# Turned tiles and decay exponents in one ring of four PSUM banks, and the next batch's q loaded earlier in two halves

## The chip, the cores and the metric

The kernel runs on one NeuronCore of a Trainium2 chip. The metric is device time in microseconds (us): how long one execution takes. A core has five engines that work in parallel, each through its own instructions in order: TensorE (PE in the profile; its weight loads are listed as PEld), VectorE (DVE), ScalarE (ACT), GpSimd (POOL) and SyncE (SP), which here does nothing but issue DMA transfers. Engines wait for each other through semaphores. TensorE writes its results to PSUM, a memory of eight banks of 2 KB per partition; VectorE and ScalarE read them from there.

## The reference

Two blocks follow one another. The first is an mLSTM cell, a recurrence over 768 positions for 4 batches and 8 heads of size 40:

```python
for t in range(S):
    m_new = np.maximum(f_gate[:, :, t] + m, i_gate[:, :, t])
    f_stab = np.exp(f_gate[:, :, t] + m - m_new)
    i_stab = np.exp(i_gate[:, :, t] - m_new)
    m = m_new
    C = f_stab[:, :, None, None] * C + i_stab[:, :, None, None] * np.einsum('bhd,bhe->bhde', vt, kt)
    n = f_stab[:, :, None] * n + i_stab[:, :, None] * kt
    h_tilde = np.einsum('bhde,bhe->bhd', C, qt)
    nq = np.einsum('bhd,bhd->bh', n, qt)[:, :, None]
    denom = np.maximum(np.abs(nq), 1.0)
    o = 1.0 / (1.0 + np.exp(-o_gate[:, :, t]))
    y[:, :, t] = o * h_tilde / denom
```

Its output, seen as 3072 rows of 320 numbers, goes through a layer of eight experts. Each row has one expert, chosen by a hash of its token id, and becomes `np.maximum(x @ w1[e], 0) @ w2[e]`, with 1024 hidden units.

## The kernel before, in words

The recurrence is computed in chunks of 128 positions: 6 chunks (`NB`) for each of 4 batches, so 24 steps `s`, with batch `b = s // 6` and chunk `c = s % 6`. The loop of line 713 issues them in an order written out by hand. The second stage, from line 775 on, runs the experts one after another on TensorE; it gathers its rows from `x_rows`, a buffer in DRAM which every step of the first stage adds 128 rows to.

One step of the loop issues, in this order:

- SyncE's loads: k for step s+3, v for step s+3 (line 164, which waits until the attention of the step before has read that buffer), in some steps a later batch's q (line 182), output gates (line 177), and one slice of expert weights (line 101).
- `decayed`: GpSimd multiplies the state C by its decay.
- `turn_k(s + 2)`: four TensorE transposes of k (line 273) and a ScalarE copy out of PSUM into `kT` (line 274). Then turns of q: `turn_q` does the same for q (lines 286 and 287). In batch 0 these are four turns of batch 0's own q in its first steps, and six turns of the next batch's q. A later batch's q lies in one tile `ql`, whose rows are interleaved, so that all six turns are needed before the first chunk of that batch can be scored. Which turns a step makes is in `first_turns` (batch 0) and `turns_of` (later batches). One step ahead of each turn `pad_q` (line 278) copies its part of `ql` into a padded tile `qp` on VectorE.
- `back(s - 1)` and `finish(s - 1)`: four transposes of the finished heads `hT` into `xo` (line 418), then VectorE and GpSimd scale them (lines 424 to 434).
- `decays(s + 1)`: four matmuls give the exponents `ab` (line 309), which ScalarE exponentiates (line 313); two more give `xb` (line 317), the weight of the state that enters the chunk. VectorE multiplies q by it into `qs` (line 321), ScalarE copies its last column to `dec` (line 323). The operand `R` of these matmuls comes from a DRAM buffer by two small transfers (`load_a`, line 197), issued on SyncE's queue one step ahead.
- `sigmoid` of the output gates on ScalarE, in steps 3, 9, 15 and 21 and once at the start; `state(s)`: sixteen matmul passes (line 376) for the update of C, which VectorE adds; the store of x (line 435); `scores(s + 1)` (line 345) and `weigh(s + 1)` on VectorE; `attend(s)` (lines 396 and 403), whose result ScalarE copies to `hT` (line 411).

In steps 2 to 22 pieces of the routing of tokens to experts lie in between, from step 13 on with matmuls into a tile `tk` (line 582).

All eight PSUM banks are in use: two for `sp0` and `sp1`, two for `ht`, two under the tag `tr` (in which `tr`, `xo`, `xb`, `tk` and some single tiles take turns) and two for `ab`. A tile in a ring of two banks waits until the tile two before it has been read.

## Time and profile before

| what | us |
|---|---|
| median of 3 runs (lowest to highest) | 449.61 (447.66 to 449.61) |
| the profiled execution: its own time | 448.97 |
| its span, first to last instruction | 447.2 |
| of this: attention loop, end of step 0's attention to end of step 23's | 33.3 to 184.0 |
| experts' matmuls | 199.5 to 439.5 |
| TensorE busy | 393.6 (88%) |
| ScalarE, VectorE, GpSimd busy | 136.3, 134.9, 118.5 |

In the chain of work that ended last, TensorE has 74% of the span; ScalarE 6%, DMA transfers 5%, SyncE's queue 3%. The parts of the profile that the prediction rests on are shown there. A timeline row gives the start, the duration, the engine, the line of the kernel, the operation with output and inputs, and in square brackets the engine's idle time before it and what ended that. A row of a table of stretches gives the stretch, its length, the busy time of TensorE, its weight loads, VectorE, ScalarE and GpSimd with their numbers of instructions, the TensorE clock that was granted (1.00 is full speed), the busy share of the 16 DMA engines, and GB/s.

### The profile page before, as it was taken

The page shows a single profiled execution, that of the slowest core. Times are in us where ns is not written, and L with a number is a line of the kernel's source. Part 1 is how long each engine was busy: PE and PEld are TensorE (multiplying, and loading weights), DVE is VectorE, ACT ScalarE, POOL GpSimd, SP SyncE. Part 2 cuts the span into 40 slices and gives each one's busy share as a digit, 9 for nine tenths or more (in the row PEclk, how much of TensorE's full clock was granted, in tenths as well). Part 3 has the DMA queues.
Part 4 walks back from the last instruction along what each step waited for, and adds up shares of the span by engine and source line. Part 5 has one row for each costly group of instructions (what it writes and reads, how often), then busy time and mean ns, then how long its engine had stood idle before and what let it go on. Part 6 is the DMA issues. An engine that isn't in the chain of part 4 may idle for free.

```text
span 447.2 us, 7391 instructions
## 1 busy us (share of the span) xinstructions
PE 393.6 (88%) x2862; PEld 263.8 (59%) x2862; DVE 134.9 (30%) x371; ACT 136.3 (30%) x238; POOL 118.5 (26%) x204
## 2 busy tenths in 40 slices
PE   3367987998899999449999999999999999999993
PEld 2255766776677787325665755655656556565551
DVE  7363544575465666211112011020020110200100
ACT  5248683576358546101111111011011111101110
POOL 6363312131233343171131240311311402011011
PEclk9989997999699999959999999999999999999997
DMA  9829569559847663143751823514417200000000
GB/s 171 208 60 177 113 140 231 108 127 220 190 116 149 141 151 94 46 118 135 250 172 29 262 77 103 177 45 133 150 45 237 88 0 31 13 15 30 1 16 28
DMA packets 111736, 51.37 MB, mean 115 GB/s; under 512 B 86576, under 2 KB 105844, under 8 KB 111700
## 3 DMA queue, kind: packets, MB, share of 16 engines
q1 hardware_dynamic: 105850, 39.31, 36.1%
q0 software_dynamic: 2496, 8.20, 5.8%
q10 hardware_dynamic: 3354, 3.37, 2.3%
q8 instruction: 23, 0.38, 0.4%
q14 instruction: 13, 0.11, 0.1%
HBM read 42.00 MB, written 8.63 MB: 113 GB/s over the span
## 4 chain that ended last, share of the span: by engine, by line
PE 74%; ACT 6%; issue 6%; DMA 5%; SPq 3%; POOL 3%; DVE 1%; ACTq 0%; POOLq 0%; DVEq 0%
PE mh L825 21%; PE zp L854 20%; PE sp L345 6%; PE mh L818 6%; PE ht L403 6%; PE ab L309 3%; PE ht L396 2%; PE xo L418 2%; PE ht L376 2%; ACT kT L274 2%; SPq L101 1%; ACT hT L411 1%; ACT qT L287 1%; PE tk L582 1%; PE tp L801 1%
## 5 line engine op out<-in xcount | busy, mean ns | idle before, releaser
L854 PE MATMUL zp<-w2t,h 128*128 128x320 f32 x384 | 105.2, 433 | 0.0
L825 PE MATMUL mh<-xT,w1t 128*128 128x416 f32 x256 | 97.9, 527 | 0.9 <-issue 0.9
L854 PEld LDWEIGHTS zp<-w2t,h 128*128 128x128 f32 x384 | 72.7, 190 | 32.1 <-issue 3.3
L825 PEld LDWEIGHTS mh<-xT,w1t 128*128 128x128 f32 x256 | 47.5, 193 | 43.8 <-issue 42.7
L807 DVE COPY xT<-tp 128x384 f32<-128x384 f32 x16 | 8.9, 558 | 141.7 <-PE tp L803 124.0
L788 POOL DMA_INDIRECT out_dram<-zo,s_idx x26 | 25.6, 986 | 92.6 <-ACT zo L787 92.6
L834 ACT ACTIVATE h<-mh 128x416 f32<-128x416 f32 x32 | 16.5, 517 | 109.2 <-PE mh L818 59.6
L787 ACT COPY zo<-zp 128x320 f32<-128x320 f32 x26 | 11.1, 425 | 101.1 <-PE zp L854 92.9
L434 POOL TENSOR_TENSOR x<-x,den 128x320 f32<-128x320 f32 x24 | 17.3, 722 | 86.4 <-DVE den L433 48.3
L353 DVE TENSOR_TENSOR w<-sp,w 128x512 f32<-128x512 f32 x48 | 30.9, 686 | 19.1 <-PE sp L345 18.0
L832 DVE TENSOR_SCALAR h<-mh 128x416 f32<-128x416 f32 x32 | 18.9, 592 | 53.4 <-PE mh L825 26.9
L345 PE MATMUL sp<-qT,kT 64*128 64x128 f32 x384 | 31.6, 310 | 3.2 <-ACT qT L287 3.2
L345 PEld LDWEIGHTS sp<-qT,kT 64*128 64x128 f32 x384 | 26.5, 210 | 5.9 <-ACT qT L287 3.6
L313 ACT ACTIVATE w<-ab 128x512 f32<-128x512 f32 x48 | 26.1, 596 | 9.6 <-PE ab L309 9.1
L403 PE MATMUL ht<-w,v 128*64 128x128 f32 x384 | 28.1, 292 | 0.0
L411 ACT COPY hT<-ht 128x512 f32<-128x512 f32 x24 | 14.0, 583 | 43.8 <-PE ht L403 39.8
L818 PE MATMUL mh<-xT,w1c 64*128 64x416 f32 x128 | 26.7, 535 | 0.0
L781 POOL DMA_INDIRECT xg<-x_rows,g_idx x24 | 23.4, 975 | 9.8 <-issue 9.8
L929 POOL COPY hrem<-h 128x256 f32<-128x256 f32 x8 | 3.2, 398 | 83.2 <-ACT h L834 83.2
L403 PEld LDWEIGHTS ht<-w,v 128*64 128x64 f32 x384 | 22.0, 144 | 4.2 <-issue 3.9
L287 ACT COPY qT<-tr 128x512 f32<-128x512 f32 x24 | 22.4, 970 | 5.1 <-PE tr L286 5.1
L286 PE MATMUL tr<-ident,qp 128*128 128x128 f32 x96 | 16.3, 298 | 8.5 <-ACT kT L274 4.4
(177 smaller groups left out, 411.7 us busy)
## 6 DMA issues: line engine op xcount, KB each, us to landing
w2t<-in_moe_w_dram SPq DMA_DIRECT2D x28, 320.0 KB
w1t<-in_moe_w_dram SPq DMA_DIRECT2D x28, 256.0 KB
k<-in_k_dram SPq DMA_DIRECT2D x24, 160.0 KB
v<-in_v_dram SPq DMA_DIRECT2D x24, 160.0 KB
og<-in_o_gate_dram SPq DMA_DIRECT2D x24, 160.0 KB
x_rows<-x SPq DMA_DIRECT2D x24, 160.0 KB
ql<-in_q_dram SPq DMA_DIRECT2D x3, 960.0 KB
w1c<-in_moe_w_dram SPq DMA_DIRECT2D x14, 128.0 KB
```

Source lines behind the costliest of these rows:

```text
L287: nc.scalar.copy(qb[b]["T"][:, :, cols], tp[:])
L313: nc.scalar.activation(w[:, hf], ab[:], AF.Exp)
L345: nc.tensor.matmul(sp[hf][:, j, :], lhsT=d["kT"][r, j, :], rhs=q_of(s)[r, j, :], start=True, stop=True,)
L353: nc.vector.tensor_tensor(d["w"][:, hf], d["sp"][hf][:], d["w"][:, hf], op=ALU.mult)
L403: nc.tensor.matmul(place(j, hf), lhsT=d["v"][:, 2 * j + hf, :], rhs=d["w"][:, hf, j, :], start=(c == 0 and j0 == 0), stop=True, skip_group ...
L411: nc.scalar.copy(d["hT"].rearrange("p f i t -> p f (i t)"), d["ht"][:, :, : 2 * P])
L781: nc.gpsimd.indirect_dma_start(out=xg, out_offset=None, in_=x_d[:, :], in_offset=bass.IndirectOffsetOnAxis(ap=idx, axis=0),)
L788: ins = nc.gpsimd.indirect_dma_start(out=out[:, :], out_offset=bass.IndirectOffsetOnAxis(ap=idx, axis=0), in_=zo[:], in_offset=None, bound ...
L818: nc.tensor.matmul(hp[i][:, :cols], lhsT=w1c[r, fp, :], rhs=xT[r, 2, :cols], start=first, stop=not first,)
L825: nc.tensor.matmul(hp[i][:, :cols], lhsT=w1t[:, db, fb * P : (fb + 1) * P], rhs=xT[:, db, :cols], start=(first and db == 0), stop=(not fir ...
L832: nc.vector.tensor_relu(h[:, 2 * fp, :cols], hp[i][:, :cols])
L854: nc.tensor.matmul(zp[:], lhsT=h[:, fb, j * P : (j + 1) * P], rhs=w[2][:, fb, :], start=(fb == 0), stop=(fb == FB - 1),)
```

## The change

There are four edits. All tiles of the tags `tr` and `ab` share one ring of four banks, in the order in which they are issued. The load of batch b+2's q, 960 KB at chunk 5, becomes two loads of four heads each, at chunks 2 and 4. The turns of q are one per step (in batch 0 two in step 4). And `decays` is cut in two: `entering`, which makes `xb`, `qs` and `dec`, comes after `state`, and `load_a` is written after it.

```diff
-        def load_q(b):
+        def load_q(b, part):
 
-            qb[b] = {"l": ld.tile([P, H, NB * D], F32, name="ql", bufs=2)}
-            nc.sync.dma_start(qb[b]["l"][:], q[b].rearrange("h (p r) d -> p h (r d)", r=NB))
+            if part == 0:
+                qb[b] = {"l": ld.tile([P, H, NB * D], F32, name="ql", bufs=2)}
+            hs = slice(part * PR, (part + 1) * PR)
+            nc.sync.dma_start(qb[b]["l"][:, hs], q[b, hs].rearrange("h (p r) d -> p h (r d)", r=NB))
...
-            tp = ps.tile([P, PR, P], F32, name="tr", tag="tr", bufs=2)
+            tp = ps.tile([P, PR, P], F32, name="tr", tag="tr", bufs=4)
...
-                ab = ps.tile([P, PR, P], F32, name="ab", bufs=2)
+                ab = ps.tile([P, PR, P], F32, name="ab", tag="tr", bufs=4)
...
-            if c > 0:
-                xb = ps.tile([P, PR, P], F32, name="xb", tag="tr", bufs=2)
+
+        def entering(s):
+            d = st[s]
+            R = Rs[s % 2]
+            if s % NB > 0:
+                xb = ps.tile([P, PR, P], F32, name="xb", tag="tr", bufs=4)
...
-        turns_of = {0: (0,), 1: (1, 2), 2: (3,), 3: (4,), 4: (5,)}
-        first_turns = {1: (0,), 2: (1, 2), 3: (3,), 4: (4, 5)}
+        turns_of = {c: (c,) for c in range(NB)}
+        first_turns = {1: (0,), 2: (1,), 3: (2,), 4: (3, 4), 5: (5,)}
...
-        load_q(1)
+        load_q(1, 0)
+        load_q(1, 1)
         gates_turn(g0)
         decays(0)
+        entering(0)
...
-            if c == 5 and b + 2 < B:
-                load_q(b + 2)
+            if c in (2, 4) and b + 2 < B:
+                load_q(b + 2, c // 2 - 1)
...
             if s + 1 < NT:
                 decays(s + 1)
-            if s + 2 < NT:
-                load_a(s + 2, nc.scalar if s == 0 else nc.sync)
...
             state(s)
             if s + 1 < NT:
+                entering(s + 1)
+                if s + 2 < NT:
+                    load_a(s + 2, nc.scalar if s == 0 else nc.sync)
                 k_weights(s + 1)
```

The other tiles of the tag `tr` (`tpg`, `xo`, `cps`, `tk`) get `bufs=4` in the same way.

## The prediction

> **What bounds the kernel now.** I read the slices of the span first, to see where TensorE is not full; the first row's digits are its busy tenths, the second the granted clock, the third the DMA share, 11.2 us per digit.

> ```profile
> PE   3367987998899999449999999999999999999993
> PEclk9989997999699999959999999999999999999997
> DMA  9829569559847663143751823514417200000000
> ```

> From the nineteenth digit on the experts keep TensorE full, which this change does not touch. Inside the loop (fourth to seventeenth digit) the clock falls twice, in the seventh and the eleventh, each time with the DMA share at 9 or 8. The chain of waits says what happens in the first (start, length, what):

> ```profile
> 64.77 0.58 SPq L182
> ...
> 65.39 0.76 SPq L177
> ...
> 66.19 1.84 SPq L177
> ...
> 68.07 3.37 SPq L101
> ...
> 71.49 2.37 DMA R<-decay_pieces
> ...
> 73.90 1.23 PE ab L309 x4
> ...
> 76.37 2.01 PE sp L345 x16
> 78.38 1.92 PE ht L403 x16
> ```

> Line 182 is batch 2's q. Behind it one weight load takes 3.37 us to issue, which took 0.61 to 0.67 in the steps beside it, so the small R transfers go out at 71.49. The matmuls at the end are slow: 2.01 and 1.92 us against 1.09 and 1.05 elsewhere in this chain. The timeline has the waits themselves:

> ```profile
> 71.72 0.33 DVE L278 COPY qp<-ql 128x320 f32<-128x320 f32 x1 [2.87 <-DMA ql<-in_q_dram]
> 72.20 0.63 PE L286 MATMUL tr<-ident,qp 128*128 128x128 f32 x4 [2.52 <-DVE qp L278]
> 73.90 1.23 PE L309 MATMUL ab<-R,L 128*64 128x512 bf16 x4 [0.64 <-DMA R<-decay_pieces]
> ```

> In an ordinary step, what TensorE waits for is ScalarE's copies, ahead of `xo` and of second turns:

> ```profile
> 88.46 0.66 PE L418 MATMUL xo<-ident,hT 128*128 128x128 f32 x4 [0.29 <-ACT kT L274]
> 81.59 0.66 PE L286 MATMUL tr<-ident,qp 128*128 128x128 f32 x4 [0.29 <-ACT kT L274]
> 82.56 0.66 PE L418 MATMUL xo<-ident,hT 128*128 128x128 f32 x4 [0.32 <-ACT qT L287]
> 45.26 0.66 PE L418 MATMUL xo<-ident,hT 128*128 128x128 f32 x4 [0.66 <-ACT qT L287]
> ```

> Last the stretches, cut at the ends of the attention of steps 4 to 12:

> ```profile
> 64.30:69.02 4.72, 4.72 (x65) 3.60 (x65) 2.31 (x7) 2.26 (x4) 1.40 (x2) 1.00 0.94 234
> 69.02:80.30 11.28, 8.11 (x69) 6.95 (x68) 5.09 (x17) 3.46 (x6) 1.86 (x3) 0.70 0.89 199
> 80.30:87.17 6.87, 6.26 (x87) 4.93 (x88) 4.05 (x15) 4.33 (x7) 1.40 (x2) 1.00 0.38 83
> 87.17:93.07 5.90, 5.61 (x83) 4.46 (x84) 3.45 (x11) 3.41 (x6) 2.63 (x5) 1.00 0.47 105
> 98.95:105.76 6.81, 5.63 (x83) 4.49 (x84) 4.10 (x13) 5.56 (x8) 0.72 (x1) 1.00 0.85 178
> 110.50:121.10 10.60, 7.91 (x67) 6.73 (x67) 4.55 (x16) 3.45 (x6) 1.40 (x2) 0.68 1.00 220
> ```

> Steps 6 and 12 (rows 2 and 6) take 11 us where others take 6, and both fill the DMA engines.

> **Part 1: q three steps sooner.** In step 6 three things go: the 2.52 us for the padded q, the 0.64 us for R, and the slow clock. From 73.90 the slow work is 1.23 (ab) + 0.28 (xb) + 0.96 (line 376) + 2.01 + 1.92 = 6.40 us; the same work at full clock, by the chain between 89.12 and 93.07, is 0.55 + 0.22 + 0.45 + 1.09 + 1.05 = 3.36. That is 3.04 us, 6.2 in all. In step 12 the waits are 1.58 and 1.11 and the slow work 6.38, so 5.7. Together 11.9 us, if nothing puts the stall elsewhere. After the change the second half is issued in step 4 (10), at about 58 us in today's clock, and is wanted by `pad_q` at the end of step 5, some 9 us later; today the whole load took 64.77 to 71.7.

> [...] The trace has 2.52 and 0.64 us of idling with 1 us of transposes between, and then 6.4 us at half rate. [...]

> **Part 2: what the halves cost on SyncE's queue.** Each half is one more issue (0.58 us by line 182's row) ahead of gates, weights and R, in steps 2, 4, 8 and 10. What a whole q costs the DMA engines follows from the stretches: steps 11 and 12 together were busy 0.87 × 4.74 + 1.00 × 10.60 = 14.7 us; two steps with their loads but no q (step 10: 0.85 × 6.81 = 5.8) are 11.6; so 3.1 us, 1.55 a half. In step 10 the queue then has 7.3 us of work in a step of about 6.3, and steps 11 and 12 have 5.8 each in about 5.1. A backlog of 1.0, then 1.7, then 2.5 us grows, and R is behind it. R goes in behind v, two gates and weights, 4.3 us of transfers (0.95 + 1.9 + 1.5, from differences between such stretches), lands about 2 us after that (2.37 by the chain, queueing included), and is wanted at 1.6 us into the next step: 6.7 us after its step began. So R is late by about half a us in each of steps 12 and 13, more if the backlog is larger. In steps 2 to 6 the same sum stays just inside. I charge 1.5 us (0 to 6), plus 0.5 for the added issues. Behind a late R on TensorE are C's update and the scores, hence everything.

> [...] I stay with 0.5. The third split, at the start, adds one issue at 13.56, where the next load but one waits till 19.65 anyway: nothing, or 0.5 us.

> **Part 3: ring and turns.** With four banks a tile waits for the fourth before it. `xo` no longer waits for the copy of kT (or of the first qT) but only for `hT`, its own input, which ScalarE has copied 0.65 us after the attention's end, while the transposes of k and q take until 1.04. New waits: the second `ab` tile waits for kT's copy (done at 1.24; it would start at about 1.9), and `xb` for qT's (done at 2.34; it starts at about 2.7, since C's update now precedes it). Both covered by 0.4 us or more; with two turns (step 4) the second `ab` is held 0.3. Full TensorE work of a step with one turn, from the chain: 0.59 + 0.45 + 0.56 + 0.55 + 0.45 + 0.22 + 1.09 + 0.60 + 1.05 = 5.56 us. From the starts of line 403:
> - steps 8 and 9: 5.90 to 5.6, 0.3 each; steps 14 and 15, with `tk` (0.68 more): 6.57 to 6.2, 0.35 each.
> - steps 10 and 16, held by the sigmoid's lateness: `xo` waits for `hT` instead of kT, 0.5 each.
> - steps 7 and 13 lose a second turn: 6.9 to 5.6, 1.3 each.
> - step 2 (three turns of q to two): 7.70 to 6.0; step 3: 6.71 to 6.0; step 4: 7.74 to 7.05; step 1: 0.9, for its third tile no longer waits behind the sigmoid (36.74 in the timeline).
> - steps 5, 11 and 17 gain a turn, and the scores that follow need its copy: 0.45 dearer each.
> - step 0: `xb` waits 3.74 us for kT with 0.81 us of C's update behind it; the update now goes first: 0.8.
> Sum: 0.6 + 0.7 + 1.0 + 2.6 + 1.7 + 0.7 + 0.7 + 0.9 - 1.3 + 0.8 = 8.4 us. Bounds: the unshown waits could take half of it; it cannot exceed TensorE's own work by more than 1.

> **Part 4: the moves.** On VectorE `qs` goes behind C's addition (0.32 us); `qs` is read by the next step's attention, a step away. On ScalarE `dec` goes behind the sigmoid; GpSimd wants it a step later, and line 382's addition waits for that, in steps that wait for the sigmoid anyhow. `load_a` passes nothing on SyncE's queue; in step 0, on ScalarE's, it passes `dec` and one load. I cost all three at nothing; without cover it is 0.3 us a step.

> **Sum.** 11.9 + 8.4 - 2.0 = 18.3 us off the profiled execution's 448.97 (span 447.2): 430.7. The median of the runs is 0.64 above that execution, so about 431.5.

> **Rivals.** (a) The stall only shrinks: the backlog of steps 10 to 12, and likewise 4 to 6, makes R late enough for the clock to fall once more. For it: those steps run the DMA engines at 0.85 to 1.00 already, and the faster loop asks for the same bytes in less time. Against it: the backlog I get is 2.5 us, spread over three steps. Each transition would lose 1.5 + 3.0 again: 440. (b) The shared ring brings nothing, because in place of waits before `xo` come waits before `ab` and `xb` on the same copies: 449.6 - 11.9 + 2 = 440. Against it: the 0.4 us of margin above. (c) Slower: the halves hold R up in all four steps in which they are issued, steps 2, 4, 8 and 10, each at today's price of 5.7 to 6.2 us: 24 us, against 11.9 + 8.4 saved, so 453. [...] (d) The load of q is not what stalls, weights are: then only part 3 counts, 441. Against it: steps 4 and 10 have gates and weights too and do not stall.

> **How the numbers follow.** Likeliest 0.62, 427 to 437; (a) 0.12; (b) 0.08; (c) 0.06; (d) 0.03; better than summed (TensorE gap-free and no late R), 423 to 427, 0.07; the rest 0.02. The range that leaves out less than 2 in 10 is 426 to 441. A measurement of this kernel can tell about 0.5%, 2.2 us, from no change: faster 0.91, within it 0.02, slower 0.07.

> **What would show it.** Right: no wait for `ql` at line 278; the clock at 1.00 in steps 5 to 13; `xo` waiting for `hT` or nothing; steps 6 and 12 at 5 us; the loop's end near 166. Wrong: matmuls of `ab` waiting for R in steps 6, 12 and 13 with a clock below 0.8 after; `ab` or `xb` waiting for kT or qT; a long issue before R in steps 2, 4, 8 or 10.

## The result, and the profile after

The changed kernel takes 430.70 us (median of four runs, 429.59 to 431.33) where the kernel before, run beside it, takes 448.74 (447.66 to 449.61): a ratio of 0.960, with a 95% interval of 0.956 to 0.963. The profiled execution took 429.59 us, its span 427.9 (before: 448.97 and 447.2). The predicted time was 431.5, with a range of 426 to 441.

The slices of the span of the changed kernel, 10.7 us per digit: TensorE's busy tenths, its granted clock and the DMA share.

```profile
PE   2369999999999992599999999999999999999992
PEclk9868999999999998589999999999999999999997
DMA  8929998899676720527616318235216201000000
```

From the fifth digit to the fifteenth TensorE is busy nine tenths of the time or more and its clock does not fall any more, although the DMA engines are busier than before (8 or 9 from the fourth digit to the tenth, where they were 5 to 9). The stretches, cut at the ends of the attention of the steps, have the columns that the prediction's table had (stretch, length, busy time of TensorE, its loads, VectorE, ScalarE, GpSimd, then clock, DMA share and GB/s); these are steps 6, 8, 12 and 13:

```profile
65.24:70.08 4.84, 4.84 (x68) 3.98 (x68) 3.79 (x14) 3.24 (x6) 1.83 (x3) 1.00 0.98 199
75.81:81.26 5.45, 5.45 (x85) 4.41 (x84) 3.57 (x12) 3.24 (x6) 2.63 (x5) 1.00 0.90 213
97.86:103.13 5.27, 5.00 (x68) 4.16 (x68) 3.23 (x13) 3.39 (x6) 1.41 (x2) 1.00 0.95 198
103.13:109.37 6.24, 5.81 (x85) 4.57 (x83) 4.58 (x14) 3.48 (x6) 2.49 (x4) 1.00 0.94 229
```

Step 6 fell from 11.19 us to 4.84, step 12 from 10.69 to 5.27, and step 8, an ordinary one, from 5.90 to 5.45 with TensorE busy in all of it. Steps 12 and 13 are not full: 0.27 and 0.43 us of them are idle.

The timeline of TensorE in the changed kernel (start, duration, line, operation, and in brackets an idle time and what ended it) shows what is left of the waits. The rows without brackets are step 9's `xo` and `xb`, which wait for nothing now. The others are waits that remain: `ab` behind two turns in step 4, the scores behind the added turn in steps 5 and 11 (and 17), and R in steps 12 and 13.

```profile
55.67 0.41 PE L311 MATMUL ab<-R,L 128*64 128x512 bf16 x2 [0.46 <-ACT qT L289]
...
62.46 1.16 PE L351 MATMUL sp<-qT,kT 64*128 64x128 f32 x16 [0.29 <-ACT qT L289]
...
82.12 0.60 PE L424 MATMUL xo<-ident,hT 128*128 128x128 f32 x4
...
83.59 0.41 PE L323 MATMUL xb<-R,Lx 128*64 128x512 bf16 x2
...
95.08 1.16 PE L351 MATMUL sp<-qT,kT 64*128 64x128 f32 x16 [0.26 <-ACT qT L289]
...
99.59 0.77 PE L311 MATMUL ab<-R,L 128*64 128x512 bf16 x4 [0.27 <-DMA R<-decay_pieces]
...
105.22 0.77 PE L311 MATMUL ab<-R,L 128*64 128x512 bf16 x4 [0.28 <-DMA R<-decay_pieces]
```

Of the signs that the prediction named, those for being right came: no wait for `ql`, the clock at 1.00 in steps 5 to 13, steps 6 and 12 near 5 us, the loop's end at 163.67. Two of those for being wrong came as well, in small: R is late in steps 12 and 13, but with no fall of the clock behind it, and `ab` waits for a copy of its ring, of kT in step 1 (0.83 us) and of qT in step 4 (0.46 us).

The chain of waits of the changed kernel (start, length, what) says why R is late in step 13. It is the last load of step 12 on SyncE's queue: v (line 164), two gates (line 177) and a weight slice (line 101) are issued first, and it goes out 4.3 us after that step began.

```profile
97.86 0.60 PE tr L275 x4
98.46 0.09 SPq L164
...
98.60 1.33 SPq L177
...
99.98 1.42 SPq L177
...
101.44 0.69 SPq L101
...
102.17 3.00 DMA R<-decay_pieces
...
105.22 0.66 PE ab L311 x4
```

**Where the time went.** The intervals between the ends of the attention give the loop: from 33.26 to 183.99 before, from 33.33 to 163.67 now, 150.73 us against 130.34. These 20.4 us are more than the span gained (19.3), because the part from the loop's end to the end of the span grew from 263.2 to 264.2. Its first group of expert matmuls is the place; from the timelines, the changed kernel first and then the one before:

```profile
179.17 5.74 PE L834 MATMUL mh<-xT,w1t 128*128 128x416 f32 x8 [0.90 <-POOL xT L896]
```

```profile
199.51 4.78 PE L825 MATMUL mh<-xT,w1t 128*128 128x416 f32 x8 [0.90 <-issue]
```

The same eight matmuls took 5.74 us instead of 4.78, for the clock, which had fallen while TensorE waited for the gathered rows, came back later in them: 5.4 us after their start instead of 3.5. In the stretches of these matmuls (the changed kernel, then the one before) the granted clock was 0.53 and 0.63:

```profile
179.17:184.91 5.74, 5.74 (x10) 2.92 (x11) 0.00 (x0) 0.00 (x0) 3.16 (x4) 0.53 0.72 251
```

```profile
199.51:204.29 4.78, 4.78 (x10) 2.54 (x11) 0.00 (x0) 0.00 (x0) 3.14 (x4) 0.63 0.92 287
```

This is not a price of the change: in the experiments below the same group takes anything from 4.62 us (the last of them) to 5.76 (q loaded whole), and the last section shows at which moments the clock changed.

### The profile page after: what moved, and what is told of

Same layout as the page of the kernel before. It is cut to its first block, busy times and chain, and to the rows that moved or that the text cites. A ratio compares the mean times of both kernels' runs of the same rounds, so it can differ in the third digit from the quotient of the medians.

```text
span 427.9 us, 7402 instructions
## 1 busy us (share of the span) xinstructions
PE 386.1 (90%) x2862; PEld 258.5 (60%) x2862; DVE 136.1 (32%) x371; ACT 134.6 (31%) x238; POOL 118.7 (28%) x204
## 3 DMA queue, kind: packets, MB, share of 16 engines
q10 hardware_dynamic: 3354, 3.37, 2.4%
## 4 chain that ended last, share of the span: by engine, by line
PE 78%; issue 5%; ACT 5%; DMA 4%; POOL 2%; DVE 1%; SPq 1%; ACTq 0%; POOLq 0%; DVEq 0%
PE mh L834 22%; PE zp L863 21%; PE mh L827 6%; PE sp L351 6%; PE ht L409 6%; PE ht L402 3%; PE ab L311 2%; PE tr L275 2%; PE xo L424 2%; PE ht L382 2%; PE tk L588 1%; PE tp L810 1%; ACT qT L289 1%; PE xb L323 1%; PE tr L288 1%
## 5 line engine op out<-in xcount | busy, mean ns | idle before, releaser
L834 PE MATMUL mh<-xT,w1t 128*128 128x416 f32 x256 | 98.9, 531 | 0.9 <-POOL xT L896 0.9
L351 PE MATMUL sp<-qT,kT 64*128 64x128 f32 x384 | 29.7, 297 | 4.1 <-ACT qT L289 4.1
L351 PEld LDWEIGHTS sp<-qT,kT 64*128 64x128 f32 x384 | 24.9, 199 | 10.8 <-ACT qT L289 6.0
L409 PE MATMUL ht<-w,v 128*64 128x128 f32 x384 | 27.1, 285 | 0.0
L275 PE MATMUL tr<-ident,k 128*128 128x128 f32 x96 | 17.2, 307 | 4.3 <-DMA k<-in_k_dram 4.3
```

Of the source, the lines that this page charges most:

```text
L275: nc.tensor.transpose(tp[:, j, :], d["k"][:, 2 * j : 2 * j + 2, :].rearrange("p h d -> p (h d)"), ident[:])
L351: nc.tensor.matmul(sp[hf][:, j, :], lhsT=d["kT"][r, j, :], rhs=q_of(s)[r, j, :], start=True, stop=True,)
L409: nc.tensor.matmul(place(j, hf), lhsT=d["v"][:, 2 * j + hf, :], rhs=d["w"][:, hf, j, :], start=(c == 0 and j0 == 0), stop=True, skip_group ...
L834: nc.tensor.matmul(hp[i][:, :cols], lhsT=w1t[:, db, fb * P : (fb + 1) * P], rhs=xT[:, db, :cols], start=(first and db == 0), stop=(not fir ...
```

## The experiments

All times are medians. The kernel before was run beside each group of four: 447.51 us (444.8 to 451.2) beside the first, 448.96 (444.6 to 450.5) beside the second, 448.62 (444.7 to 451.3) beside the third. The step lengths come from the profiled execution of each kernel. The changed kernel itself was run only for the result above (430.70 us); from one group to the next the kernel before moves by up to 1.5 us, so a difference of that size from 430.70 tells nothing by itself.

### The load alone

The kernel before, with q in halves at chunks 2 and 4.

```diff
-            if c == 5 and b + 2 < B:
-                load_q(b + 2)
+            if c in (2, 4) and b + 2 < B:
+                load_q(b + 2, c // 2 - 1)
```

> The kernel before with the load of q alone changed (two halves, at chunks 2 and 4). My theory: the two stalls of steps 6 and 12 go, nothing else does, so about 11 us less than before: 438. Rival, that the ring and the turns carry the gain and the stall would have gone elsewhere: 445 or more, with TensorE waiting for R in steps 6 and 12 and a clock near 0.7 there.

Measured: 439.75 us, ratio 0.981 (0.972 to 0.989). Steps 6 and 12 took 5.30 us each where they took 11.19 and 10.69, with no wait for `ql` or R; steps 7 and 13 became 0.2 us dearer. So it was q's load that stalled the loop, not the weights that go through the queue at the same time: rival (d) is out.

### The change without its load

The changed kernel with one load of q at chunk 5, the same diff the other way round.

> The changed kernel with the load of q back at chunk 5 in one piece. My theory: both stalls return at 5.5 to 6 us each, so about 11 us more than the changed kernel: 442. Rival, that ring and turns alone hide the load: under 435.

Measured: 436.15 us, ratio 0.971 (0.963 to 0.979). Both stalls are back (TensorE idle for 1.70 and 0.54 us in step 6, 1.30 and 0.86 in step 12), but step 6 took 10.29 us at a clock of 0.67 and step 12 took 7.36 at 1.00. On top of the rest of the change the load is worth 5 to 6 us, alone 7.8. The forecast, 442, had both stalls at the full price; in the profiled execution one of them came without a fall of the clock.

### The ring alone

The kernel before, with four banks for `tr` and `ab` together.

```diff
-            tp = ps.tile([P, PR, P], F32, name="tr", tag="tr", bufs=2)
+            tp = ps.tile([P, PR, P], F32, name="tr", tag="tr", bufs=4)
-                ab = ps.tile([P, PR, P], F32, name="ab", bufs=2)
+                ab = ps.tile([P, PR, P], F32, name="ab", tag="tr", bufs=4)
```

> The kernel before with the shared ring of four banks alone; loads, turns and the order of xb as before. My theory: the waits ahead of xo go, 0.3 us in a step with one turn, 0.8 in one with two or three, some 6 to 7 us over the loop: 442. Rival, that new waits ahead of ab and xb take their place: 448 to 450. The two stalls stay in both.

Measured: 445.32 us, ratio 0.993 (0.988 to 0.997). Steps 8 and 9 took 5.85 and 5.87 us, where they had taken 5.90 and 5.91: hardly anything gained. (Steps 1 to 3 together gained 2.1 us.) Its timeline in step 9 shows where the wait went:

```profile
90.20 0.60 PE L418 MATMUL xo<-ident,hT 128*128 128x128 f32 x4
90.73 0.62 PE L309 MATMUL ab<-R,L 128*64 128x512 bf16 x4
91.65 0.41 PE L317 MATMUL xb<-R,Lx 128*64 128x512 bf16 x2 [0.29 <-ACT qT L287]
```

`xo` no longer waits, and `xb`, the fourth tile after q's turn, waits the same 0.29 us for the copy of that turn. That is rival (b), and for the ring by itself, in the ordinary steps, it was right.

### The turns alone

The kernel before, with one turn of q per step.

```diff
-        turns_of = {0: (0,), 1: (1, 2), 2: (3,), 3: (4,), 4: (5,)}
+        turns_of = {c: (c,) for c in range(NB)}
```

and `first_turns` as in the change.

> The kernel before with one turn of q per step alone. My theory: steps 7 and 13 lose about 1 us each, step 2 nearly as much, steps 5, 11 and 17 gain 0.5 each: 1 to 2 us less, 447. Rival, that the turns and not the ring bring what the loop gains outside the stalls: 441.

Measured: 441.92 us, ratio 0.988 (0.978 to 0.998), nearer to the rival's 441. Yet the turns themselves nearly cancel: steps 2, 7 and 13 gained 1.0, 0.6 and 0.8 us, steps 5, 11 and 17 lost 0.9, 0.6 and 0.8. What it gained came from steps 6 and 12, 7.41 and 7.49 us long: TensorE waited there too (1.59 and 0.43, 1.21 and 0.95 us), but its clock stayed at 1.00.

### q loaded whole

The changed kernel, with one load of 960 KB at chunk 2.

```diff
-            if c in (2, 4) and b + 2 < B:
-                load_q(b + 2, c // 2 - 1)
+            if c == 2 and b + 2 < B:
+                load_q(b + 2)
```

> The changed kernel with q loaded at chunk 2 in one piece. By my sum the split costs one issue of 0.5 us and a whole q puts 3.1 us of transfers ahead of R in steps 2 and 8 instead of 1.55 in each of 2, 4, 8, 10; both steps have room, steps 10 to 12 get lighter, so the late R of steps 12 and 13 shrinks: 0.5 to 1 us less than the changed kernel, 430. If halves were needed to let R pass: R late in steps 3 and 9, 433 or more. [...]

Measured: 429.71 us, ratio 0.957 (0.953 to 0.961), as the theory had it: one us below the changed kernel, which is within the noise between groups. The late R has moved from steps 12 and 13 to steps 3 and 9, which follow the load; in the timeline of this kernel:

```profile
49.13 0.78 PE L309 MATMUL ab<-R,L 128*64 128x512 bf16 x4 [0.35 <-DMA R<-decay_pieces]
...
84.08 0.59 PE L309 MATMUL ab<-R,L 128*64 128x512 bf16 x3 [0.71 <-DMA R<-decay_pieces]
```

These steps took 6.40 and 6.48 us instead of 5.93 and 5.45. Splitting the load was not needed; loading it sooner was. (Whether chunk 3 or 4 would have been soon enough was not tried.)

### R first in its step

The changed kernel, with the two small transfers of R ahead of the other loads of a step.

```diff
             b, c = s // NB, s % NB
+            if 0 < s and s + 2 < NT:
+                load_a(s + 2, nc.sync)
             if 0 < s < NT - 3:
                 load_k(s + 3)
...
                 entering(s + 1)
-                if s + 2 < NT:
-                    load_a(s + 2, nc.scalar if s == 0 else nc.sync)
+                if s == 0:
+                    load_a(2, nc.scalar)
```

> The changed kernel with the two R transfers issued first in each step, ahead of k, v, q, gates and weights. My theory: the late R of steps 12 and 13 (0.27 and 0.28 us of waiting in the profile) goes, and what TensorE loses there in all is 0.5 to 0.7 us: 430. Rival, that the queue as a whole is short and something else becomes late instead (k, gates or x): no change or 0.5 us more.

Measured: 428.12 us (427.44 to 428.62), ratio 0.954 (0.950 to 0.958), with all six runs below the four of the changed kernel, which were made on another occasion. Step 12 fell from 5.27 to 4.84 us and step 13 from 6.24 to 5.74; the other steps from 2 on are within 0.03. That puts the late R at 0.93 us, where the prediction charged 1.5. Something else came late in its place once, as the rival had it: TensorE waits 0.20 us for k in step 13. The remaining 1.6 us between the two medians are not in the steps. The two profiled executions are 2.15 us apart, and 1.1 of that lie in the first group of expert matmuls, which took 4.63 us here instead of 5.74, the clock having come back sooner (in the eighteenth of the forty slices of the span the granted clock is 0.9 or more here, and in the 0.8s in the changed kernel); so not all of the 2.6 us can be credited to R.

### R first in the kernel before

The same edit on the kernel before.

> The kernel before with the two R transfers first in each step; q still loaded at chunk 5. The waits for R in steps 6 and 12 (0.64 and 1.11 us) go, the waits for the padded q (2.5 and 1.6) stay. If the clock falls for the padded q's wait alone, 1.8 us less than before: 447. [...]

Measured: 445.89 us, ratio 0.993 (0.990 to 0.996), 1.1 us under the forecast and 3.1 under the kernel before. The wait for R is gone in both steps, but the waits for the padded q stay, in the timeline:

```profile
74.93 0.63 PE L286 MATMUL tr<-ident,qp 128*128 128x128 f32 x4 [2.42 <-DVE qp L278]
...
114.42 0.63 PE L286 MATMUL tr<-ident,qp 128*128 128x128 f32 x4 [2.44 <-DVE sl_i L553]
```

and its stretches for steps 6 and 12 are:

```profile
71.91:80.96 9.05, 6.63 (x69) 5.30 (x68) 4.18 (x14) 3.31 (x6) 1.86 (x3) 0.81 0.92 209
111.39:119.18 7.79, 5.17 (x68) 4.08 (x68) 3.56 (x13) 3.32 (x6) 1.40 (x2) 1.00 0.92 207
```

Two waits of the same length, 2.42 and 2.44 us, in steps of nearly the same work: one cost clock (0.81 over the step) and one did not (1.00). The R wait is not what made the difference; the last section sets the two beside twelve others.

### xb ahead of C's update

The changed kernel, with `entering` back at its old place in the order.

```diff
             if s + 1 < NT:
                 decays(s + 1)
+                entering(s + 1)
...
             if s + 1 < NT:
-                entering(s + 1)
                 if s + 2 < NT:
```

> The changed kernel with xb made right after the exponents again, ahead of the update of C. It then comes at about 2.25 us into a step and its bank is free at 2.34 (the copy of qT): 0.1 us a step in some 15 steps, 1 to 1.5 us more than the changed kernel, 432. Rival, that the move is worth nothing: within 0.5 us.

Measured: 434.64 us, ratio 0.969 (0.965 to 0.973): 4 us lost, three times what was expected. Steps 8 and 9 are at 5.87 and 5.86 us, as with the ring alone, and for the same reason:

```profile
86.47 0.41 PE L323 MATMUL xb<-R,Lx 128*64 128x512 bf16 x2 [0.29 <-ACT qT L289]
```

### The move alone, and ring and move together

Of the three edits apart from the load, neither the ring alone nor the turns alone made the ordinary steps 8 and 9 shorter (5.85 and 5.87; 5.90 each). That left the move, alone and with the ring. First the kernel before, with `entering` split off and put behind `state`:

```diff
             if s + 1 < NT:
                 decays(s + 1)
-            if s + 2 < NT:
-                load_a(s + 2, nc.scalar if s == 0 else nc.sync)
...
             state(s)
             if s + 1 < NT:
+                entering(s + 1)
+                if s + 2 < NT:
+                    load_a(s + 2, nc.scalar if s == 0 else nc.sync)
                 k_weights(s + 1)
```

> The kernel before with the move alone: xb, qs and dec behind the update of C, load_a behind them; ring of two, old turns, old load. Theory (move and ring pay only together): in a ring of two the second tile of the step is xo, and it still waits 0.29 us for the copy of kT, so the single-turn steps 8 and 9 stay at 5.9 us and the time stays within 1 us of the kernel before, up to the size of its two stalls. Rival (the move alone frees TensorE of something): steps 8 and 9 at 5.5 and the time 6 to 10 us less.

Measured: 444.73 us, ratio 0.994 (0.991 to 0.998), which is 3.9 us less than before, not within 1. Steps 8 and 9 stayed at 5.91 and 5.90, with `xo` still waiting 0.29 us for kT; steps 3, 4 and 10, held by the sigmoid, gained 0.3 to 0.4 each. Most of the profiled execution's gain is again in steps 6 and 12: 8.37 and 9.63 us, of which more below.

Then the same with the ring of four:

> The kernel before with the ring of four and the move of xb behind C's update; old turns, old load. Theory: the ring takes the wait for kT from xo and the move takes the wait for qT from xb, so steps 8 and 9 fall from 5.9 to 5.45 us, as in the changed kernel, where the ring alone left them at 5.85: over some 20 steps 5 to 8 us under the ring alone, so 438 to 441, with the two stalls still there. Rival (the turns of q one per step are needed as well): as with the ring alone, 445.

Measured: 436.39 us, ratio 0.976 (0.971 to 0.982), below the forecast of 438 to 441; in four of six runs 436.1 to 436.5, in the other two 440.2 and 441.6 (the profiled one). Steps 8 and 9 took 5.43 and 5.44 us, `xo` and `xb` without a wait. In medians the ring alone gave 2.2 us, the move alone 3.9, both together 12.2. The medians also hold the stalls, whose price differs from run to run. That ring and move work only together is shown by the ordinary steps, which gained 0.04, 0.0 and 0.47 us, and by all of the loop but steps 6 and 12, which is 3.0 us shorter than before with the ring alone, 1.2 with the move alone and 8.8 with both. With the turns as well (the change without its load) it was 436.15: the turns add nothing to the pair that can be measured.

### The turn of q ahead of the turn of k at chunk 5

On top of R first, `turn_k` goes behind the turn of q in steps 5, 11 and 17.

```diff
-            if s + 2 < NT:
+            if s + 2 < NT and c < 5:
                 turn_k(s + 2)
...
                     turn_q(b + 1, r, slice(r, None, NB))
+            if s + 2 < NT and c == 5:
+                turn_k(s + 2)
```

> The changed kernel with R issued first in its step and, in the steps of chunk 5, the turn of q ahead of the turn of k. Theory: the scores of steps 5, 11 and 17 wait 0.28, 0.25 and 0.29 us for ScalarE's copy of qT only because the copy of kT is ahead of it; the wait goes and the time is 0.8 us less than with R first alone: 427.3, with these steps at 5.2, 4.8 and 5.5 us. Rival (the next thing in that step, xo behind hT or C's update, takes the wait over): no change from R first alone, 428.1.

Measured: 428.21 us, ratio 0.956 (0.951 to 0.961): no gain over R first alone, as the rival had it, with another wait than it named. Steps 5 and 17 gained 0.15 and 0.20 us, step 11 lost 0.29, since the padded q was not ready when its turn came first:

```profile
93.46 0.63 PE L288 MATMUL tr<-ident,qp 128*128 128x128 f32 x4 [0.44 <-DVE qp L280]
```

VectorE makes it behind the products of the scores. The turn of k had been the work that covered this.

### All of it with q whole

The run before it, with one load of q at chunk 2.

> As the run before it (R first, turn of q ahead of the turn of k at chunk 5), but q loaded whole at chunk 2 instead of in halves at chunks 2 and 4. Theory: the halves matter only through what R waits behind; with R first in its step nothing waits behind q, and the two are equal within 0.5 us: 427.3, no R wait in steps 3 and 9. Rival (the whole load holds up gates or weights or the next R): steps 3 and 9 dearer by 0.5 to 1.0 us each, as with the whole q alone, so 428.8.

Measured: 428.26 us, ratio 0.957 (0.952 to 0.962); steps 3 and 9 at 5.92 and 5.45, with no wait for R. With R first, whole or halved is the same. R first on the changed kernel (428.12) and the last two cannot be told apart; all three are 2.4 to 2.6 us under the changed kernel.

## Why the prediction was right, point by point

The prediction took 18.3 us off the profiled execution; the changed kernel's profiled execution is 19.4 us shorter. The terms of the sum, against the lengths of the steps in the two profiles:

| term | predicted, us | measured, us |
|---|---|---|
| Part 1: stalls of steps 6 and 12 | 11.9 | 6.35 + 5.85 = 12.2 (step 12 without the late R, 10.69 - 4.84) |
| Part 2: late R | -1.5 | -0.93 (R first: 0.43 + 0.50) |
| Part 2: added issues | -0.5 | 0 seen |
| Part 3: steps 8 to 10, 14 to 16 | 2.3 | 0.45 + 0.46 + 0.73 + 0.47 + 0.45 + 0.76 = 3.3 |
| steps 7 and 13 | 2.6 | 1.14 + 1.16 = 2.3 (step 13 without the late R) |
| steps 1 to 4 | 4.0 | 1.41 + 1.66 + 0.78 + 0.80 = 4.65 |
| steps 5, 11, 17 | -1.3 | -0.74 - 0.45 - 0.67 = -1.9 |
| step 0 | 0.8 | -0.1 |
| steps 18 to 23 | 0 | 0.7 |
| from the loop's end on | 0 | -1.0 |

**Part 1** was right in mechanism and in size for the profiled execution, with the slow clock's 6.1 us (3.04 and 3.02) taken from the rows. As the price of the stall in general it was too high: the load alone gave 7.8 us in medians, and 5 to 6 on top of the rest. The kernel before is itself 444.6 to 451.3 us from run to run, and its profiled execution had both stalls at the highest price that any profile here shows. The last section sets the prices side by side. So it is in part luck that the sum came within 1 us of the measured median: in medians the load's term was 4 to 6 us too large, and the rest too small, since without the load the change gave 11.4 us (447.51 less 436.15) where Part 3 had 8.4.

**Part 2.** The backlog was where the sum put it, in steps 12 and 13, and TensorE waited 0.27 and 0.28 us for R, half of the half us that was worked out. (By the sum's own figures only step 12 is late by half a us; with a backlog of 1.7 us step 13 would be late by 1.3, and it was not.) The cost was 0.43 and 0.50 us, more than the two waits: the matmuls just behind a late R also take longer, 1.36 and 1.37 us from the start of `ab` to that of the scores, where they take 1.27 and 1.22 with R first. Rival (a) needed the clock to fall there; it stayed at 1.00. Rival (c) needed late R in steps 3, 5, 9 and 11: there was none with the halves, and even the whole load made it 0.71 us at most. In the change without its load, waits of 1.70 and 0.54 us in step 6 came with a fall, to a clock of 0.67 over the step; the 2.52 and 0.64 us of the kernel before came with 0.69. The added issues show nowhere: the 0.5 us for them was an estimate from line 182's row, and no run shows it.

**Part 3** gave 8.9 us where it had 8.4, and 1.4 more than it had if step 0 is left out. Ordinary steps went to 5.45 us where the sum of the chain's pieces was 5.56. But its margin was wrong. The text had `xb` covered by 0.4 us: copy of qT done at 2.34 us after the attention's end, `xb` due at 2.7. The copy was timed well: where `xb` waits for it, with the ring alone, it starts at 2.31 (91.65 less 89.34). But in the changed kernel `xb` starts 2.33 us after the attention's end (83.59 less 81.26), because TensorE runs through the step without holes. The cover is 0.02 us, and it exists only because C's update goes ahead of `xb`. The prediction did count on that order, and in **Part 4** it put the moves at nothing; undone, the move takes 4 us away. So rival (b), given 0.08, was one edit away.

**Step 0** was wrong, by its own 0.8 us. C's update does go ahead now and `xb` waits at 28.78 as before, but in the profiled execution what follows lost to the clock what had been saved; the last attention matmuls in the changed kernel, then in the one before, by their timelines and stretches:

```profile
31.36 1.97 PE L409 MATMUL ht<-w,v 128*64 128x128 f32 x16
...
31.36:33.33 1.97, 1.97 (x19) 1.64 (x18) 1.52 (x3) 0.03 (x1) 1.19 (x7) 0.50 0.24 38
```

```profile
32.04 1.22 PE L403 MATMUL ht<-w,v 128*64 128x128 f32 x16
...
32.04:33.26 1.22, 1.22 (x19) 1.05 (x18) 1.05 (x2) 0.00 (x0) 0.65 (x2) 0.88 0.94 170
```

They start 0.68 us sooner and take 0.75 us longer: the clock rose at 34.4 us in the changed kernel, at 32.3 in the one before. Where it rose at 32.2 and 32.7 with the move (the move alone; the turn of q first), step 0 ended at 32.94 and 32.93; in the five kernels without the move in which it rose at 32.3 to 32.7, at 33.26 to 33.45. So the saving is there, 0.3 to 0.5 us of the 0.8, and the clock took it back.

## What to carry to other kernels

Follow a wait to the next tile before calling it gone: a ring with more banks moves a producer's wait to the tile that is now that many behind it, and here it paid (0.47 us in an ordinary step against 0.04) only with independent work, C's update, ahead of that tile too. Put small transfers that gate the next step first on their queue, ahead of the large ones that are wanted later (0.93 us here). And when a stall drops TensorE's clock, one profile shows one price of it (the same two waits below went with steps of 11.19, 8.37 and 9.87 us); look at several executions, or several kernels with the same stall, before taking that price as its value, and cut the trace at the moments at which the clock changed, as below, to compare a stall that cost little with one that cost much.

## What the runs showed of the hardware

| kernel, step | idle, us | length, us | clock | half-clock time, us | busy in the interval, us | in the next, us |
|---|---|---|---|---|---|---|
| before, 6 | 2.52 + 0.64 | 11.19 | 0.69 | 6.9 | 1.06 | 2.82 |
| before, 12 | 1.58 + 1.11 | 10.69 | 0.68 | 6.8 | 1.19 | 2.96 |
| change without load, 6 | 1.70 + 0.54 | 10.29 | 0.67 | 6.8 | 1.60 | 2.99 |
| change without load, 12 | 1.30 + 0.86 | 7.36 | 1.00 | 0 | 1.77 | |
| ring alone, 6 | 2.96 | 9.43 | 0.82 | 3.4 | 0.85 | 3.02 |
| ring alone, 12 | 2.19 + 1.10 | 11.32 | 0.70 | 6.8 | 1.06 | 2.86 |
| turns alone, 6 | 1.59 + 0.43 | 7.41 | 1.00 | 0 | 1.87 | |
| turns alone, 12 | 1.21 + 0.95 | 7.49 | 1.00 | 0 | 1.73 | |
| before with R first, 6 | 2.42 | 9.05 | 0.81 | 3.4 | 1.21 | 3.42 |
| before with R first, 12 | 2.44 | 7.79 | 1.00 | 0 | 1.70 | |
| move alone, 6 | 2.53 + 0.57 | 8.37 | 1.00 | 0 | 1.73 | |
| move alone, 12 | 1.97 + 0.84 | 9.63 | 0.82 | 3.5 | 1.29 | 3.41 |
| ring and move, 6 | 2.49 + 0.59 | 9.87 | 0.83 | 3.4 | 1.51 | 3.42 |
| ring and move, 12 | 2.46 + 1.04 | 11.50 | 0.70 | 6.9 | 1.06 | 2.92 |

Three of them have the same two waits, 2.5 and 0.6 us in step 6. The kernel before took 11.2 us (the stretch shown in the prediction is cut a little wider); the timelines and stretches of the other two, the move alone and then ring and move:

```profile
70.88 0.63 PE L286 MATMUL tr<-ident,qp 128*128 128x128 f32 x4 [2.53 <-DVE qp L278]
```

```profile
67.75:76.12 8.37, 5.26 (x69) 4.25 (x68) 4.09 (x14) 3.46 (x6) 1.87 (x3) 1.00 0.94 205
```

```profile
68.42 0.63 PE L286 MATMUL tr<-ident,qp 128*128 128x128 f32 x4 [2.49 <-DVE qp L278]
```

```profile
65.34:75.21 9.87, 6.79 (x67) 5.51 (x68) 4.19 (x14) 3.46 (x6) 1.87 (x3) 0.83 0.95 219
```

TensorE's busy time is 8.02 us in step 6 of the kernel before, 5.26 with the move and 6.79 with ring and move, for the same matmuls. The half-clock times of the table lie at 0, at 3.4 to 3.5 and at 6.8 to 6.9 us and nowhere between.

The traces show when the clock changed. In that of the kernel before it changed nine times from 28.93 us on, in that of the changed kernel seven times from 17.35 on, and each change comes a whole number of intervals of 3.413 us after every other one of its trace. Where the intervals begin differs from trace to trace: counted from the first instruction, the first boundary comes at 0.3 us in the changed kernel's, at 1.6 in that of the kernel before, at 2.3 in that of ring and move. The table's last two columns are TensorE's busy time in the interval of the stall and, where that was followed by half clock, in the next. Cut at these boundaries, the three stalls look like this (the columns of the stretches again; the kernel before, the move alone, ring and move):

```profile
69.89:73.30 3.41, 1.06 (x8) 0.96 (x9) 1.41 (x6) 0.90 (x2) 0.00 (x0) 1.00 0.72 167
73.30:76.72 3.42, 2.82 (x26) 2.54 (x27) 1.85 (x6) 1.86 (x4) 1.40 (x2) 0.50 1.03 199
76.72:80.13 3.41, 3.41 (x32) 2.94 (x30) 1.67 (x5) 0.00 (x0) 0.46 (x1) 0.50 0.89 217
```

```profile
66.35:69.77 3.42, 1.99 (x36) 1.41 (x28) 1.18 (x2) 1.16 (x2) 0.59 (x1) 1.00 1.06 282
69.77:73.18 3.41, 1.73 (x16) 1.49 (x17) 2.25 (x10) 1.07 (x2) 0.12 (x1) 1.00 0.64 169
```

```profile
63.70:67.11 3.41, 2.23 (x38) 1.64 (x36) 1.29 (x2) 1.16 (x2) 0.83 (x2) 1.00 1.12 304
67.11:70.52 3.41, 1.51 (x12) 1.22 (x14) 2.25 (x10) 1.05 (x1) 0.00 (x0) 1.00 0.64 172
70.52:73.94 3.42, 3.42 (x37) 2.97 (x33) 1.02 (x2) 1.25 (x3) 1.87 (x3) 0.50 1.15 230
```

In the fourteen stalls of the table, transposes counted as work, the nine intervals with at most 1.60 us of busy TensorE were each followed by half clock, and the five with 1.70 us or more were not. Of the nine intervals at half clock that came next, the four with at least 3.02 us of work were followed by full clock, and the five with at most 2.99 us by another one at half. The traces of the kernel before and of the changed kernel, cut at all their boundaries from the first recorded change on, have 242 pairs of neighbouring intervals: the nine falls in them follow 0 to 1.19 us of work, full clock goes on after 1.99 us or more, the seven rises follow 3.41 us, and half clock goes on after 2.96 us or less. These are busy times of the profile, which models the ends of matmuls, and no run here shows more than these cases.

So the same wait cost nothing where a boundary divided it well (the move alone, 1.99 and 1.73 us of work on its two sides), one interval at half clock where the next interval was full of work (ring and move, 3.42 us), and two where the wait for R fell into that next interval (the kernel before, 2.82 us). The longest idle time in the table is 2.96 us, and the price is one of three. In time, taken as half of the half-clock time, the three are 0, 1.7 and 3.4 us; over the fourteen stalls the mean is 1.7, half of what the profile of the kernel before shows for each of its two.

The moments at which the clock came back in step 0 and in the first expert group lie on the same boundaries: 32.34 and 203.01 us in the kernel before, 34.41 and 184.60 in the changed kernel. The boundaries would also fit the 6.7 us over which the kernel before scatters in its runs, against 1.7 us, in fewer runs, for the changed kernel, which has no such stall in its loop; but only one execution of each was profiled, so this last part stays an argument.
